# A first product's bank copied by ScalarE, and weight and activation sums moved, in a fused attention and feed-forward kernel

## The chip, the cores and the metric

The kernel runs on one core of one Trainium2 chip. The metric is the device time of one execution in microseconds. Before the change the median of three runs is 286.3 us (286.28 to 286.6). The profile that is read here is of one execution, with a span of 284.8 us from the first to the last instruction and a mean granted TensorE clock of 1.000.

## The reference

Pooled attention for 8 batches of 8 heads, 576 tokens and head size 64 (keys and values are averaged over groups of 8 tokens, which leaves 72), then a feed-forward layer with the gate h * cos(h) on all 4608 tokens:

```python
k_p = k.reshape(B, H, Sp, pool, D).mean(axis=3)          # Sp = 72, pool = 8
v_p = v.reshape(B, H, Sp, pool, D).mean(axis=3)
scores = scale * np.matmul(q, k_p.transpose(0, 1, 3, 2))
attn = softmax(scores)                                   # written out in the reference
attn_out = np.matmul(attn, v_p)

x = attn_out.transpose(0, 2, 1, 3).reshape(B * S, H * D) # 4608 x 512
h = x @ w_in                                             # 512 x 2048
g = h * np.cos(h)
out = g @ w_out                                          # 2048 x 512, float32
```

## The kernel before

The tokens are worked through in nine tiles of 512 (`t` = 0 to 8). In a tile, an "up" matmul makes h in eight blocks; ScalarE takes the cosine of each block and VectorE multiplies, which gives `g_sb`. A "down" matmul follows. While tile t is in its down matmul, the attention of batch t + 1 is computed between its parts. The order of the program is the order in which each engine works (the kernel uses a manual schedule).

From tile 1 on, the down matmul is done as a Strassen-Winograd scheme: seven products of half-size blocks instead of eight, at the price of sums of blocks. Sums of weights (`w1` to `w4`, made once, in two halves each) and of activations (`g1` to `g4`, in every tile, in two halves each) are inputs of the products:

```python
def put_weights(i, eng, ks=(1, 3, 2, 4)):
    (b11, b12), (b21, b22) = [(w[:, :, 0:HM], w[:, :, HM:]) for w in (w_out_sb[i], w_out_sb[i + 2])]
    for k in ks:
        out, x, y, op = {1: (w1, b12, b11, SUB), 3: (w3, b22, b12, SUB), 2: (w2, w3[i], b11, ADD),
                         4: (w4, b21, w2[i], SUB)}[k]
        eng.tensor_tensor(out=out[i], in0=x, in1=y, op=op)                       # L387

def put_g(k, i):
    f0, f1 = 4 * i, 4 * i + 4
    t1f1, t1f2, t2f1, t2f2 = [g_part(f, t, f0, f1) for t in range(2) for f in range(2)]
    out, x, y, op = {1: (g1, t2f1, t2f2, ADD), 2: (g2, g1[:, f0:f1], t1f1, SUB), 3: (g3, t1f1, t2f1, SUB),
                     4: (g4, t1f2, g2[:, f0:f1], SUB)}[k]
    nc.vector.tensor_tensor(out=out[:, f0:f1], in0=x, in1=y, op=op)              # L397
```

The seven products share two PSUM banks, A and Bb. Each product is 16 matmuls (L431). The first and third product both start a new sum in A, the second and fourth in Bb; between them the bank is read out:

```python
products = [
    (A, True, part(g_part(0, 0, 0, HF)), of(w_out_sb[0:2])),     # product(0)
    (Bb, True, part(g_part(1, 0, 0, HF)), of(w_out_sb[2:4])),    # product(1)
    (A, True, part(g2), of(w2)),                                 # product(2)
    (Bb, True, part(g1), of(w1)),                                # product(3)
    (A, False, part(g3), of(w3)),
    (Bb, False, part(g4), of(w_out_sb[2:4], 1)),
    (A, False, part(g_part(1, 1, 0, HF)), of(w4)),
]
# ... cut ...
            if other is None:
                (nc.scalar.copy if t >= B - 1 else nc.vector.tensor_copy)(out=out[:, p, m], in_=ps)   # L445
            else:
                nc.vector.tensor_tensor(out=out[:, p, m], in0=ps, in1=other[:, p], op=ADD)            # L447
# ... cut ...
reads = [
    lambda: each(p1, A),                  # reads[0]: the only plain copy; p_sb in the profile
    lambda: each(o1, Bb, p1, m1, 0),      # reads[1]
    lambda: each(v16, A, p1),             # reads[2]
    # ... four more, cut ...
]
```

The down part of tiles 1 to 8, with the attention between the products (`steady` is true in tiles 1 to 6, `rest` in 1 to 7). `scores_mm` are matmuls (L233), `scores_exp` is an exponential on ScalarE (L240), `values_rows` is matmuls (L295), a reciprocal and a multiplication on VectorE and a transpose by DMA:

```python
def scores_of(*parts):
    for part in parts:
        scores_mm(*part)
    for part in parts:
        scores_exp(*part)
# ... cut ...
if rest:
    exp_tables()
product(0)
product(1, 0, 2)
if steady:
    scores_of(u0, u1, u2)
elif rest:
    scores_of(ur)
product(1, 2)
if t == 1:
    put_g(2, 0)
put_gs((1, 1), (2, 1))
reads[0]()
if not steady:
    reads[1]()
put_gs((3, 1), (4, 1))
if steady:
    reads[1]()
    values_rows(*u0)
if t == 1:
    put_g(4, 0)
product(2)
reads[2]()
# ... cut: products 3 to 6 with the rest of the attention ...
```

Tile 0 has an ordinary down matmul (L370). Its attention steps and half of the weight sums stand between its matmuls; `fill` is a list of (place, step), where the place counts the 64 matmuls. The other half of the weight sums is done by GpSimd, which also pools the keys and values (L156, L162, L165, L168) and issues their loads:

```python
fill = [(2, fill[0][1]), (2, S_(0, 0)), (8, lambda: pool_v_mm(1, banks[1])),
        (8, lambda: values(t, REST, banks[2])), (8, S_(1, 0)), (8, V_(0, 1)),
        (18, S_(2, 2)), (21, V_(1, 0, later)), (26, S_(3, 1)), (32, lambda: later.pop()()),
        (32, V_(2, 2)), (40, V_(3, 0))]
# ... cut ...
    if n == 4:
        put_weights(0, nc.vector, (1,))
    elif n == 36:
        put_weights(1, nc.vector, (3,))
put_weights(1, nc.vector, (2, 4))
# ... cut: end of the tile ...
if t == 0:
    load_kv(b + 1, "k", k)
    load_q(b + 1)
    load_kv(b + 1, "v", v)
    put_weights(0, nc.gpsimd, (3, 2, 4))
    put_weights(1, nc.gpsimd, (1,))
# ... cut ...
pool_first(b + 1, "k")
if t != 1 and b + 2 < B:
    load_kv(b + 2, "k", k)
pool_rest(b + 1, "k")
```

Of the kernel before, what the change touches and what calls it, by code (L numbers as in the profile page):

```python
# [20 lines left out]
def kernel(  # L21
# [9 lines left out]
    nc = tc.nc  # L31
    B, H, S, D = q.shape
# [370 lines left out]
    def down_products(t):  # L403

        def of(w, m=0):
            return lambda fc: w[fc // 4][:, fc % 4, m * HM:(m + 1) * HM]

        def part(x):
            return lambda fc, p: x[:, fc, p * 128:(p + 1) * 128]

        apart = t == NT - 1
        if apart:
            A, Bb = [[x[:, 0:HM] for x in two] for two in (obanks, (banks[1][:, 0, :], banks[2][:, 0, :]))]
        else:
            A, Bb = [[obanks[i][:, p * HM:(p + 1) * HM] for p in range(2)] for i in (1, 0)]
        products = [
            (A, True, part(g_part(0, 0, 0, HF)), of(w_out_sb[0:2])),
            (Bb, True, part(g_part(1, 0, 0, HF)), of(w_out_sb[2:4])),
            (A, True, part(g2), of(w2)),
            (Bb, True, part(g1), of(w1)),  # L420
# [4 lines that stand above are left out]
        mms = []  # L425
        for n, (bank, first, g, w) in enumerate(products):
            order = [(fc, p) for fc in range(HF) for p in range(2)]
            if apart and n == 6:
                order.sort(key=lambda x: x[1])
            for fc, p in order:  # L430
                mms.append(lambda bank=bank, first=first, g=g, w=w, fc=fc, p=p: nc.tensor.matmul(  # L431
                    bank[p], lhsT=g(fc, p), rhs=w(fc),
                    start=(first and fc == 0 and (apart or p == 0)), stop=(fc == HF - 1 and (apart or p == 1)),
                    skip_group_check=not first))

        p1, v16, q15 = [msb.tile([128, 2, HM], FP32, name=n, tag=n, bufs=1) for n in ("p1_sb", "v_sb", "q_sb")]
        o1, o2 = [msb.tile([128, 2, d_model], FP32, name="o_two", tag="o_two", bufs=2) for _ in range(2)]
        m1, m2 = slice(0, HM), slice(HM, d_model)

        def each(out, bank, other=None, m=slice(0, HM), tk=None):  # L440

            for p in range(2) if apart else (slice(0, 2),):
                ps = bank[p] if apart else obanks[1 if bank is A else 0].rearrange("p (a m) -> p a m", a=2)
                if other is None:
                    (nc.scalar.copy if t >= B - 1 else nc.vector.tensor_copy)(out=out[:, p, m], in_=ps)  # L445
                else:
                    nc.vector.tensor_tensor(out=out[:, p, m], in0=ps, in1=other[:, p], op=ADD)  # L447
                if apart and tk is not None:
                    rows_out(t, tk, out, (p,), m, (nc.sync, nc.scalar))

        reads = [
            lambda: each(p1, A),
            lambda: each(o1, Bb, p1, m1, 0),
            lambda: each(v16, A, p1),
            lambda: each(q15, Bb, p1),
            lambda: each(o2, A, q15, m2, 1),
            lambda: (each(o1, Bb, v16, m2, 0), apart or stores.append(lambda: rows_out(t, 0, o1))),
            lambda: (each(o2, A, p1, m1, 1), apart or stores.append(lambda: rows_out(t, 1, o2))),
        ]
        return [mms[i * 2 * HF:(i + 1) * 2 * HF] for i in range(7)], reads  # L460
# [100 lines left out]
    for t in range(NT):  # L561
# [5 lines left out]
        for n, fp in enumerate(up_order(t)):  # L567
            up_mm(t, fp, 2 if n < 2 else 0)
            between = ()
            if t == 0:  # L570
                if fp == 4:
                    puts = pool_k_mm(1, obanks[0], 0, 2), pool_k_mm(1, obanks[1], 2, 4)
                elif fp in (5, 6):
                    g0 = 9 * (fp - 5)
                    puts = q_transpose_mm(1, obanks[0], g0, g0 + 5), q_transpose_mm(1, obanks[1], g0 + 5, g0 + 9)
                if fp in (4, 5, 6):
                    puts[0](vec)
                    between = ((puts[1], act),)
            up_g(t, fp, between)
            if 0 < t and 3 <= n < 6:  # L580
                put_gs(*[(k, 0) for k in (((3,), (1,), ()) if t == 1 else ((1, 2), (3,), (4,)))[n - 3]])
            if 0 < t and b < B:
                if n == 0:
                    q_transpose(b)
                    k_transpose(b)
                elif n == 2:
                    pool_rest(b, "v")
                    if b + 1 < B:
                        nc.gpsimd.tensor_copy(out=gate, in_=kk[b % 2][0:1, H - 1, 0:1])
                        load_q(b + 1)  # L590
                        load_kv(b + 1, "v", v)
            if n == 2:
                while stores:
                    stores.pop(0)()
# [17 lines left out]
            fill = [(1, lambda: scores(t, REST, banks[2])), (16, lambda: values(t, REST, banks[1]))]  # L612
        if t == 0:
            fill = [(2, fill[0][1]), (2, S_(0, 0)), (8, lambda: pool_v_mm(1, banks[1])),
                    (8, lambda: values(t, REST, banks[2])), (8, S_(1, 0)), (8, V_(0, 1)),
                    (18, S_(2, 2)), (21, V_(1, 0, later)), (26, S_(3, 1)), (32, lambda: later.pop()()),
                    (32, V_(2, 2)), (40, V_(3, 0))]
        if t == FIRST:
            early_inverses.clear()
        if t < FIRST:  # L620
            fi = 0
            for n, (ms, fc) in enumerate(mms):
                while fi < len(fill) and fill[fi][0] <= n:
                    fill[fi][1]()
                    fi += 1
                down_mm(obanks[ms % 2], ms, fc)
                if fc == FFCH - 1:
                    down_out(t, ms, obanks[ms % 2])
# [6 lines that stand above are left out]
            products, reads = down_products(t)  # L635

            def product(i, j=0, k=2 * HF):
                for mm in products[i][j:k]:
                    mm()

            later = []

            u0, u1, u2, u3 = [(b, CHUNKS[i], banks[j]) for i, j in enumerate((2, 1, 0, 1))]
            ur = (t, REST, banks[2])
# [7 lines that stand above are left out]
            def muls():  # L652
                while later:
                    later.pop(0)()

            steady, rest = b < B, t < B
# [12 lines that stand above are left out]
            reads[0]()  # L669
            if not steady:  # L670
                reads[1]()
            put_gs((3, 1), (4, 1))
            if steady:
                reads[1]()
                values_rows(*u0)
            if t == 1:
                put_g(4, 0)
            product(2)
            reads[2]()
            if steady:  # L680
                values_rows(*u1)
                values_rows(*u2)
            product(3)
            reads[3]()
            muls()
            product(4)
            reads[4]()
            muls()
            if steady:
                scores_of(ur, u3)  # L690
            product(5, 0, 4)
            if rest:
                values(*ur, later)
            product(5, 4, 12)
            muls()
            if steady:
                values_rows(*u3)
            product(5, 12)
            reads[5]()
            muls()  # L700
            product(6)
            reads[6]()
        if t < B:
            sin_tables()
        if b + 1 < B:
            if t == 0:
                load_kv(b + 1, "k", k)
                load_q(b + 1)
                load_kv(b + 1, "v", v)
                put_weights(0, nc.gpsimd, (3, 2, 4))  # L710
                put_weights(1, nc.gpsimd, (1,))
            else:

                nc.gpsimd.tensor_copy(out=gate, in_=g4[0:1, HF - 1, 0:1])  # L714
# [35 lines left out]
```

The softmax here doesn't subtract the row's maximum and nothing guards it: scores larger than these inputs give would overflow.

## Time and profile before

| quantity | value |
|---|---|
| time, median of three runs | 286.3 us |
| span of the profiled execution | 284.8 us |
| TensorE busy | 276.2 us |
| VectorE busy | 215.3 us |
| ScalarE busy | 164.4 us |
| GpSimd busy | 143.4 us |
| copy of A to p_sb on VectorE (128x512 float32), tiles 1 to 6 | 0.68 us each |
| copy of A to p_sb on ScalarE, tile 7 (same shape) | 0.57 us |
| weight sum on GpSimd | 2.13 us each, four |
| weight sum on VectorE | 0.68 to 2.28 us, four |

An engine's busy time is the sum over the whole span. The page splits the span into engines, groups of instructions by line and shape, and the chain of waits: the steps that, followed back from the last instruction, released one another. Timelines of a stretch show single instructions with start and length in microseconds; where instructions of one line follow closely they are merged, with their number behind the x. A tile's length is read from the starts of two up matmuls (L353) that follow one another.

### The profile page before, as it was taken

How to read it: one execution, taken by the hardware profiler on the slowest of the kernel's cores; microseconds unless marked ns; L12 is line 12 of the kernel's file. 1: busy time of each engine (PE TensorE's matmuls, PEld its weight loads, DVE VectorE, ACT ScalarE, POOL GpSimd, SP SyncE). 2: the span in 40 equal slices, each digit the busy share in tenths (PEclk: the TensorE clock that was granted, in tenths of full speed). 3: DMA queues.
4: the chain of work that ended last, by engine and by line, in shares of the span. 5: the costliest groups of instructions: out<-in, count | busy, mean ns of one | idle time of the engine just before them, and what ended most of it. 6: DMA issues, size and time to landing. Idle time of an engine off the chain costs nothing.

```text
span 284.8 us, 5857 instructions
## 1 busy us (share of the span) xinstructions
PE 276.2 (97%) x2360; PEld 176.4 (62%) x2360; DVE 215.3 (76%) x314; ACT 164.4 (58%) x193; POOL 143.4 (50%) x150
## 2 busy tenths in 40 slices
PE   7889999999999999999999999999999999999994
PEld 2545554446874587458745884588458844874583
DVE  5448757899957995699569956995699569856972
ACT  3787798367257735674567556655656555436600
POOL 8553069996599259924993499439900000000000
PEclk9999999999999999999999999999999999999999
DMA  7999999793939698998678969882670261015014
GB/s 154 202 206 207 207 205 216 118 199 54 145 48 161 124 221 135 138 166 169 104 135 152 186 90 160 146 172 57 119 153 3 55 128 40 0 24 126 2 37 111
DMA packets 57738, 36.12 MB, mean 127 GB/s; under 512 B 35441, under 2 KB 53361, under 8 KB 57713
## 3 DMA queue, kind: packets, MB, share of 16 engines
q0 software_dynamic: 19744, 18.07, 41.1%
q1 hardware_dynamic: 37328, 17.18, 30.0%
q10 hardware_dynamic: 640, 0.52, 0.8%
q8 instruction: 18, 0.29, 0.4%
q14 instruction: 8, 0.06, 0.1%
HBM read 36.70 MB, written 9.44 MB: 162 GB/s over the span
## 4 chain that ended last, share of the span: by engine, by line
PE 86%; DVE 6%; ACT 3%; DMA 2%; issue 1%; POOL 0%; DVEq 0%; POOLq 0%; ACTq 0%
PE bank L353 35%; PE obank L431 32%; PE obank L370 4%; PE obank L353 4%; PE bank L233 3%; DVE g_sb L367 3%; DMA q_b<-in_q_dram 2%; PE bank L295 2%; PE bank L431 2%; PE bank L268 1%; DVE w L387 1%; DVE g L397 1%; ACT cos L363 1%; ACT ex L240 1%; DVE vz L187 0%
## 5 line engine op out<-in xcount | busy, mean ns | idle before, releaser
L353 PE MATMUL bank<-xT,w_in_sb 128*128 128x512 bf16 x512 | 114.0, 379 | 0.2 <-DVE g_sb L367 0.2
L363 ACT ACTIVATE cos<-bank,half_pi 128x1024 f32<-128x1024 f32 x64 | 70.4, 1114 | 56.9 <-PE bank L353 55.0
L353 PEld LDWEIGHTS <-w_in_sb 128*128 128x128 bf16 x576 | 56.1, 98 | 66.2 <-issue 0.9
L367 DVE TENSOR_TENSOR g_sb<-bank,cos 128x1024 bf16<-128x1024 f32 x64 | 77.1, 1219 | 25.1 <-ACT cos L363 24.9
L156 POOL TENSOR_TENSOR half_sums<-kv_st 72x512 f32<-72x512 bf16 x48 | 54.7, 1165 | 0.6 <-issue 0.2
L240 ACT ACTIVATE ex<-bank 72x1024 bf16<-72x1024 f32 (+1 forms) x40 | 35.0, 929 | 34.0 <-PE bank L233 33.8
L431 PEld LDWEIGHTS <-g 128*128 128x128 bf16 x512 | 47.9, 98 | 6.1 <-issue 0.3
L431 PE MATMUL obank<-w,g 128*128 128x256 bf16 x368 | 42.7, 272 | 0.2 <-DVE p_sb L445 0.2
L431 PEld LDWEIGHTS <-g_sb 128*128 128x128 bf16 x384 | 36.8, 98 | 6.9 <-DVE g_sb L367 0.3
L162 POOL TENSOR_TENSOR half_sums<-half_sums 72x512 f32<-72x512 f32 x24 | 30.4, 1288 | 0.0
L431 PE MATMUL obank<-w_out_sb,g_sb 128*128 128x256 bf16 x240 | 28.9, 273 | 0.0
L397 DVE TENSOR_TENSOR g<-g_sb 128x1024 bf16<-128x1024 bf16 x32 | 23.3, 728 | 0.5
L714 POOL COPY gate<-g 1x1 bf16<-1x1 bf16 x5 | 0.9, 179 | 34.1 <-DVE g L397 34.1
L279 DVE TENSOR_TENSOR xT<-bank,inv 64x256 bf16<-64x256 f32 x14 | 5.9, 422 | 15.0 <-ACT inv L275 14.9
L300 DVE TENSOR_TENSOR x_rows<-bank,inv_rows 128x512 bf16<-128x512 f32 x24 | 16.6, 691 | 0.8
L431 PE MATMUL obank<-w_out_sb,g 128*128 128x256 bf16 x112 | 15.6, 273 | 0.0
L431 PE MATMUL obank<-w,g_sb 128*128 128x256 bf16 x128 | 15.3, 273 | 0.0
L370 PE MATMUL obank<-w_out_sb,g_sb 128*128 128x512 bf16 x64 | 15.2, 379 | 0.0
L353 PE MATMUL obank<-xT,w_in_sb 128*128 128x512 bf16 x64 | 15.1, 379 | 0.0
L233 PE MATMUL bank<-qT,kk 64*72 64x128 bf16 (+2 forms) x288 | 12.7, 221 | 0.1
L233 PEld LDWEIGHTS <-kk 64*72 64x72 bf16 x288 | 8.8, 110 | 5.3 <-issue 3.8
L331 ACT ACT_TABLE_LOAD x9 | 11.5, 1283 | 0.9 <-PEq L734 0.7
(103 smaller groups left out, 277.1 us busy)
## 6 DMA issues: line engine op xcount, KB each, us to landing
out_dram<-o_two SPq DMA_DIRECT2D x64, 128.0 KB, 2.4
kv_st<-in_v_dram POOLq DMA_DIRECT2D x8, 576.0 KB, 11.2
kv_st<-in_k_dram POOLq DMA_DIRECT2D x7, 576.0 KB, 8.5
q_b<-in_q_dram POOLq DMA_DIRECT2D x6, 576.0 KB, 7.5
w_in_sb<-in_moe_w_in_dram POOLq DMA_DIRECT2D x4, 512.0 KB, 13.5
w_out_sb<-in_moe_w_out_dram POOLq DMA_DIRECT2D x4, 512.0 KB, 18.2
q_b<-in_q_dram POOLq DMA_DIRECT2D x4, 288.0 KB, 12.4
g_sb<-in_k_dram SPq DMA_DIRECT2D x1, 576.0 KB, 3.6
```

The source lines that it names most:

```text
L156: nc.gpsimd.tensor_tensor(out=s[:, h:h + 2], in0=x[:, h:h + 2, 0:4, :], in1=x[:, h:h + 2, 4:8, :], op=ADD)
L162: add(out=s[:, h:h + 4, 0:2, :], in0=s[:, h:h + 4, 0:2, :], in1=s[:, h:h + 4, 2:4, :], op=ADD)
L233: nc.tensor.matmul(pair[:Sp, bank, c:c + n].rearrange("p (g n) -> p g n", n=64), lhsT=kk[b % 2][half[r], key_slot(b, h0 + i, r), 0:Sp], rh ...
L240: nc.scalar.activation(out=ex[:, 0:nh * n].rearrange("p (a n) -> p a n", a=2), in_=pair[:Sp, :, 0:nh * n // 2], func=ACTF.Exp, scale=scale ...
L300: nc.vector.tensor_tensor(out=x[0:n].rearrange("p (j a d) -> p j a d", j=KCH, a=2), in0=ps[0:n, :, 0:2 * (D + 2)].rearrange("p j (a w) -> ...
L331: nc.scalar.preload_act_table_set("natural_log_exp_and_others")
L353: nc.tensor.matmul(h[j] if h is obanks else h[:, j, :], lhsT=w_in_sb[fc // 4][:, ki, (fc % 4) * 128:(fc % 4 + 1) * 128], rhs=xT[:, ki, t * ...
L363: nc.scalar.activation(out=c, in_=ps, func=ACTF.Sin, bias=half_pi[:, :1])
L367: nc.vector.tensor_mul(out=o, in0=ps, in1=c)
L370: nc.tensor.matmul(o, lhsT=g_sb[:, fc, ms * 128:(ms + 1) * 128], rhs=w_out_sb[fc // 4][:, fc % 4, :], start=(fc == 0), stop=(fc == FFCH - 1))
L397: nc.vector.tensor_tensor(out=out[:, f0:f1], in0=x, in1=y, op=op)
L431: mms.append(lambda bank=bank, first=first, g=g, w=w, fc=fc, p=p: nc.tensor.matmul(bank[p], lhsT=g(fc, p), rhs=w(fc), start=(first and fc ...
```

## The change

Three things are moved; the arithmetic stays. The plain copy of bank A is made by ScalarE in every tile, so that VectorE has one instruction less in each of tiles 1 to 6. The four weight sums that GpSimd made are made by VectorE in tile 0, at places where it waits for others, so that GpSimd can begin to pool the next keys earlier. In tiles 1 and 2 the activation sums come later in the up matmul, and g4's first half after it, so that the products that the up matmul waits for come ahead of them.

```diff
                 if other is None:
-                    (nc.scalar.copy if t >= B - 1 else nc.vector.tensor_copy)(out=out[:, p, m], in_=ps)
+                    nc.scalar.copy(out=out[:, p, m], in_=ps)
@@
             up_g(t, fp, between)
-            if 0 < t and 3 <= n < 6:
-                put_gs(*[(k, 0) for k in (((3,), (1,), ()) if t == 1 else ((1, 2), (3,), (4,)))[n - 3]])
+
+            sums = {0: {}, 1: {5: (1,), 6: (3,)}, 2: {4: (1, 2), 5: (3,)}}.get(t, {3: (1, 2), 4: (3,), 5: (4,)})
+            put_gs(*[(i, 0) for i in sums.get(n, ())])
@@
             fill = [(2, fill[0][1]), (2, S_(0, 0)), (8, lambda: pool_v_mm(1, banks[1])),
-                    (8, lambda: values(t, REST, banks[2])), (8, S_(1, 0)), (8, V_(0, 1)),
-                    (18, S_(2, 2)), (21, V_(1, 0, later)), (26, S_(3, 1)), (32, lambda: later.pop()()),
+                    (8, lambda: values(t, REST, banks[2])),
+                    (8, lambda: put_weights(0, nc.vector, (3, 2))), (8, S_(1, 0)), (8, V_(0, 1)),
+                    (18, S_(2, 2)), (18, lambda: put_weights(0, nc.vector, (4,))),
+                    (18, lambda: put_weights(1, nc.vector, (1,))), (21, V_(1, 0, later)), (26, S_(3, 1)), (32, lambda: later.pop()()),
                     (32, V_(2, 2)), (40, V_(3, 0))]
@@
             reads[0]()
             if not steady:
                 reads[1]()
-            put_gs((3, 1), (4, 1))
+            put_g(3, 1)
+            if t == 1:
+                reads[1]()
+            if t <= 2:
+                put_g(4, 0)
+            put_g(4, 1)
             if steady:
-                reads[1]()
+                if t > 1:
+                    reads[1]()
                 values_rows(*u0)
-            if t == 1:
-                put_g(4, 0)
             product(2)
@@
                 load_kv(b + 1, "v", v)
-                put_weights(0, nc.gpsimd, (3, 2, 4))
-                put_weights(1, nc.gpsimd, (1,))
```

## The prediction

> **What bounds the kernel now.** I read the page's header parts first, then the idle time of TensorE, then the chain of waits, and only then the timelines of single tiles. The page's first part says which engine is full:
>
> ```profile
> PE 276.2 (97%) x2360; PEld 176.4 (62%) x2360; DVE 215.3 (76%) x314; ACT 164.4 (58%) x193; POOL 143.4 (50%) x150
> ```
>
> TensorE (PE) is busy for 276.2 of 284.8 us; 8.6 us of idle is all that any rearrangement of the other engines can win. I asked for the busy time by stretch, with the borders put where each tile's up matmul starts. Columns after the border: length of the stretch, then busy time and instruction count of PE, of weight loads, of VectorE (DVE), ScalarE (ACT), GpSimd (POOL), then clock and DMA.
>
> ```profile
> 0.00:17.40 17.40, 13.80 (x173) 7.44 (x174) 9.47 (x22) 10.71 (x14) 11.37 (x23) 1.00 1.03 183
> ...
> 53.40:83.10 29.70, 29.24 (x257) 19.50 (x256) 27.01 (x35) 17.05 (x19) 24.39 (x23) 1.00 0.73 118
> 83.10:112.20 29.10, 29.07 (x258) 19.30 (x256) 23.25 (x35) 17.05 (x19) 20.02 (x21) 1.00 0.95 150
> ...
> 141.10:170.06 28.96, 28.96 (x258) 19.41 (x256) 23.03 (x35) 17.05 (x19) 19.56 (x21) 1.00 0.81 142
> ...
> 254.60:284.80 30.20, 26.03 (x176) 16.98 (x174) 19.70 (x30) 9.61 (x11) 0.00 (x0) 1.00 0.32 70
> ```
>
> Idle TensorE lies in the first stretch (17.40 - 13.80 = 3.6 us) and the last (30.20 - 26.03 = 4.2 us), neither of which the change touches. Tile 4 (141.10 to 170.06) has none. Tile 1 (53.40 to 83.10) has 0.46 us, tile 2 has 0.03 us. By the starts of the up matmuls in the PE timeline (53.20, 82.98, 112.00, 140.95 us) tile 1 takes 29.78 us, tile 2 29.02 and tile 3 28.95. So the change can win at most 0.83 us in tile 1 and 0.07 in tile 2, some 0.9 us or 0.3%.
>
> The chain of waits over 53 to 76 us shows where tile 1 loses it. Columns: start, length, what.
>
> ```profile
> 54.09 2.21 DVE w L387
> ...
> 56.32 1.65 DVE w L387
> ...
> 65.68 1.90 PE bank L353 x8
> ...
> 71.91 0.61 DVE p_sb L445
> 72.52 0.04 issue
> 72.56 1.91 PE obank L431 x16
> ```
>
> Two weight sums hold VectorE back by 3.9 us, its products come late, and TensorE waits twice for 0.23 us: at 65.68 for a g_sb product, at 72.56 for the copy of the first product's bank. The second wait also tells a dependency that matters below: **the third product (L431, x16, operand w2) cannot start before p_sb is copied**, because it starts a new sum in the bank that the copy reads. It follows the copy's end by 0.04 us.
>
> In steady tiles this copy is just in time. Tile 4, the timeline of all engines from 156 to 160 us, where the last line is cut by the window (start, busy time, engine, line, operation):
>
> ```profile
> 156.09 1.28 ACT L331 ACT_TABLE_LOAD   x1
> ...
> 157.39 2.84 ACT L240 ACTIVATE ex<-bank 72x1024 bf16<-72x1024 f32 x3
> ...
> 158.70 0.68 DVE L445 COPY p_sb<-obank 128x512 f32<-128x512 f32 x1
> 159.27 0.41 PE L295 MATMUL bank<-vz,ex 72*128 72x65 bf16 x8
> ...
> 159.52 0.71 PE L431 MATMUL obank<-w,g 128*128 128x256 bf16 x5
> ```
>
> VectorE's copy ends at 159.38 and the third product starts at 159.52: 0.14 us of slack. And ScalarE is in the middle of three exponentials until 160.23. The reader should hold those two numbers side by side.
>
> **What the Trainium skill says.** "PSUM — Partial Sum Buffer", section Engine vs sequencer instructions: "ScalarE/VectorE/GpSimdE queues are strict FIFO." The trace agrees as far as it can: in each tile the records of an engine stand in the order of the program. "SBUF — State Buffer", section Who interferes with whom, has a VectorE instruction with two SBUF inputs exclude a GpSimd instruction that reads SBUF, the later one waiting for the whole of the other. The trace agrees: the weight sum takes 0.68 us at 36.1 while GpSimd is idle, but 2.28 at 54.0 and 1.65 at 56.3, while GpSimd runs its float32 sums (L162, L165). "ScalarE: Activation LUTs", section Table sets: the hidden batching unit, lists copy among the functions of every set, so a copy on ScalarE needs no table load; in tile 7, where ScalarE already makes it, it follows the exponential with no load between.
>
> **The change part by part.**
>
> *The copy on ScalarE.* In tiles 7 and 8 it is there already; so six tiles change, 1 to 6. It takes 0.68 us off VectorE and puts this on ScalarE (row of tile 7):
>
> ```profile
> 244.23 0.59 ACT L240 ACTIVATE ex<-bank 72x512 bf16<-72x512 f32 x1
> 244.72 0.57 ACT L445 COPY p_sb<-obank 128x512 f32<-128x512 f32 x1
> ```
>
> It lasts 0.57 us and starts 0.10 before the recorded end of the exponential ahead (244.23 + 0.59 - 244.72). In tile 7 there is one exponential ahead of it, in tiles 1 to 6 there are three: in the program scores_of(u0, u1, u2) issues all of them before reads[0]. That order is not changed. So in tile 4 the copy starts at 157.39 + 2.84 - 0.10 = 160.13, ends at 160.70, and the third product may start at 160.74 instead of 159.52: **TensorE stands still for 1.22 us.** Tile 3 gives the same (exponentials at 128.44, product at 130.57: 131.79 - 130.57 = 1.22). TensorE has no idle time later in the tile in which to make that up, and the next tile's table load, exponentials and copy all follow TensorE, so it comes back each tile. Tiles 3 to 6: 4 x 1.22 = 4.9 us.
>
> *Tile 2.* A steady tile plus the stall, 28.95 + 1.22 = 30.17, against 29.02 now: +1.15. The later g4 sum takes away the 0.07.
>
> *Tile 1.* Sums moved later (g1 and g3 after the sixth and seventh block of the up matmul, one after the other, instead of the fourth and fifth) let the products of blocks 5 to 7 go ahead; the sum at 62.68, which cost 1.81 us beside GpSimd, goes to a quieter place. That should remove the wait at 65.68. If tile 1 then keeps the pace of tile 3, where the exponentials start 128.44 - 112.00 = 16.44 after the up matmul, they start at 69.64, the copy ends at 69.64 + 2.84 - 0.10 + 0.57 = 72.95, and the third product starts at 72.99 against 72.56: +0.43. If nothing is recovered they start at 70.03 and it is +0.82. I take +0.6.
>
> *Weight sums on VectorE.* Four GpSimd sums of 2.13 us go, four VectorE sums come, 0.68 each with GpSimd idle, 4 x 0.68 = 2.7 us. Two go into the hole between 39.88 and 41.81 (1.93 us against 1.36), two into that between 43.20 and 44.54 (1.34 against 1.36). Just about fits; the copy of the first output block behind the second hole may come 0.1 late, and with it TensorE at 47.57, where it already follows a VectorE product. I put +0.1 on it, up to +0.3.
>
> *GpSimd freed.* This looks like 8.5 us (four sums from 38.55 to 47.14), but the first pooling sum behind them needs keys whose transfer was issued at 25.98 and took 20.5 us to land: 46.5. GpSimd starts its pooling 0.6 us earlier at most, so its float32 sums still meet the two weight sums left at the end of tile 0, and those stay near 3.9 us.
>
> Sum: 4.9 + 1.15 + 0.6 + 0.1 = 6.7 us; 286.3 + 6.7 = 293.0 us.
>
> **The rivals.** (a) *The relief counts, the copy is free.* If ScalarE made the copy before or between the exponentials, TensorE would lose nothing and up to 0.9 us would be won: 285.4 to 286.3. For it: ScalarE is only 58% busy and idle after its exponentials. Against: program order, and that the bank is wanted 0.7 us before the exponentials end. Average load hides this. (b) *The freed GpSimd brings transfers forward* and they collide with the transposes and stores. The late key transfer speaks against it; effect under 0.5 us either way. (c) *VectorE becomes the bound in tile 0*: two weight sums more before the end of tile 0 lengthen the chain of attention values. VectorE is busy 9.23 of 14.5 us there; even if all of the second pair fell on the path, 1.4 us, total near 294.3. (d) *The stall is smaller than worked out*, because TensorE catches up elsewhere. The windows show no idle in tiles 3 to 6, so nothing can be caught up.
>
> **Range and chances.** The main term is 1.22 us with about 0.1 either way, six times: 0.6 us. Tile 1 adds 0.2, tile 0 up to 0.3 either side. Range 291.9 to 293.9 us. The border of 2% slower lies at 286.3 x 1.02 = 292.0, 1.0 below my figure, so most of the range is beyond it: slower by over 2% 0.85, within 2% 0.13. Faster by over 2% would need more than the 0.9 us to be won: 0.02.
>
> **What would show it.** Right: p_sb's copy on ScalarE directly behind the three exponentials, ending some 3.3 us after the first of them started; in tiles 1 to 6 a wait of TensorE L431 on ACT p_sb L445 of about 1.2 us each (7 us in all, tile 1 included); tiles 3 to 6 each 30.2 us long; TensorE's busy time unchanged at 276 and the span about 291.5. Tile 1: no wait for g_sb. Tile 0: weight sums of 0.7 us. Wrong: a copy that stands before an exponential, a third product that starts without it, or a tile 3 of 28.95 us. If tile 3 is 30.2 and the total still differs, the fault is in tiles 0 to 2.

## The result, and the profile after

The changed kernel takes 295.59 us (median of four runs, 295.3 to 295.94) against 286.45 us for the kernel before: a ratio of 1.0314 (95% interval 1.0291 to 1.0337), 9.1 us slower. The predicted direction holds; the predicted time, 293.0 us with a range up to 293.9, was too low. The profiled execution has a span of 293.5 us, 8.7 more than before. The first part of the page after:

```profile
PE 276.9 (94%) x2360; PEld 176.8 (60%) x2360; DVE 214.0 (73%) x312; ACT 167.1 (57%) x199; POOL 133.7 (46%) x146
```

VectorE has become lighter (215.3 to 214.0 us), GpSimd too (143.4 to 133.7), TensorE does the same work in 8.7 us more. The totals would be read as relief; only TensorE's idle time tells. Its waits over the whole span (who waited for whom: total, times, longest), the two that are new:

```profile
PE obank L431 <- ACT p_sb L445: 6.2, 6, 1.1
PE bank L353 <- DVE o_two L447: 1.6, 1, 1.6
```

Six waits for ScalarE's copy, and one wait of an up matmul, which was not foreseen. By stretch, cut where the up matmuls of tiles 1, 2, 3 and 4 and of the last tile start (columns as in the prediction):

```profile
53.08:83.25 30.17, 29.17 (x257) 19.51 (x256) 25.29 (x35) 17.50 (x20) 23.43 (x22) 1.00 0.74 117
83.25:115.41 32.16, 29.33 (x259) 19.29 (x257) 24.13 (x36) 17.51 (x20) 22.91 (x26) 1.00 0.97 147
115.41:145.58 30.17, 29.10 (x257) 19.48 (x258) 20.99 (x31) 17.51 (x20) 18.28 (x20) 1.00 0.84 130
145.58:175.75 30.17, 29.10 (x259) 19.50 (x256) 22.60 (x34) 17.51 (x20) 19.71 (x21) 1.00 0.81 137
262.73:293.50 30.77, 26.21 (x178) 17.10 (x175) 19.71 (x30) 9.60 (x11) 0.00 (x0) 0.98 0.31 69
```

Tiles 1, 3 and 4 (and 5 and 6) are 30.17 or 30.18 us long: the 28.95 of a steady tile before and 1.22. Tile 2 is 32.16. The last stretch is 30.77, where it was 30.32 before (from 254.43 to 284.75). Tile 4, ScalarE's and TensorE's instructions from 162 to 166 us, the last cut by the window:

```profile
162.02 2.84 ACT L240 ACTIVATE ex<-bank 72x1024 bf16<-72x1024 f32 x3
...
163.90 0.41 PE L295 MATMUL bank<-vz,ex 72*128 72x65 bf16 x8
...
164.74 0.58 ACT L445 COPY p_sb<-obank 128x512 f32<-128x512 f32 x1
...
165.38 0.82 PE L431 MATMUL obank<-w,g 128*128 128x256 bf16 x6 [1.07 <-ACT p_sb L445]
```

The copy stands behind the three exponentials and ends at 165.32; the third product follows at 165.38, and the bracket says that TensorE was idle for 1.07 us before it. The tile grows by 1.22: in the row of before, the records of the value matmuls (L295) and of the third product overlap by 0.16 us (159.27 + 0.41 - 159.52), and behind a wait that overlap is lost.

Tile 2's extra length lies at its end. There the profile names the VectorE sum of L447 as what the up matmul waited for. The transfers issued between 108.0 and 108.2 us say something else (output, queue, count, size, median us from issue to landing):

```profile
kv_st<-in_k_dram POOLq DMA_DIRECT2D x1, 576.0 KB, 8.9
xT<-x_rows SPq DMA_TRANSPOSE x1, 7.1
```

The transpose of the third chunk of batch 3's tokens into xT starts at 108.07 and lands 7.1 us later, at 115.2; the up matmul of tile 3, which reads these tokens, starts at 115.41. Before, the same transpose, issued between 107.03 and 107.6, took 2.5:

```profile
xT<-x_rows SPq DMA_TRANSPOSE x1, 2.5
```

What differs is the load of keys (kv_st, 576 KB). Before, it was issued 0.65 us behind the last transpose:

```profile
107.03 1.22 SPq L304 DMA_TRANSPOSE xT<-x_rows  x1
107.68 0.84 POOL L115 DMA_DIRECT2D kv_st<-in_k_dram  x1 [0.30 <-POOL half_sums L156]
```

After, the two are issued together:

```profile
108.07 1.22 SPq L304 DMA_TRANSPOSE xT<-x_rows  x1
108.09 0.84 POOL L115 DMA_DIRECT2D kv_st<-in_k_dram  x1 [0.30 <-POOL half_sums L156]
```

That suggested the second theory below.

### The profile page after: what moved, and what is told of

Its sections match the earlier page's. It is cut to its first block, busy times and chain, and to the rows that moved or that the text cites. A ratio compares the mean times of both kernels' runs of the same rounds, so it can differ in the third digit from the quotient of the medians.

```text
span 293.5 us, 5838 instructions
## 1 busy us (share of the span) xinstructions
PE 276.9 (94%) x2360; PEld 176.8 (60%) x2360; DVE 214.0 (73%) x312; ACT 167.1 (57%) x199; POOL 133.7 (46%) x146
## 4 chain that ended last, share of the span: by engine, by line
PE 77%; ACT 10%; DVE 6%; issue 3%; DMA 2%; POOL 0%; DVEq 0%; POOLq 0%; ACTq 0%
PE bank L353 36%; PE obank L431 24%; ACT ex L240 6%; PE obank L353 5%; PE obank L370 4%; DVE g_sb L367 3%; ACT cos L363 3%; DMA q_b<-in_q_dram 2%; PE bank L431 2%; PE bank L233 1%; PE bank L295 1%; PE bank L268 1%; ACT p_sb L445 1%; DVE o_two L447 1%; DVE g L397 1%
## 5 line engine op out<-in xcount | busy, mean ns | idle before, releaser
L367 DVE TENSOR_TENSOR g_sb<-bank,cos 128x1024 bf16<-128x1024 f32 x64 | 77.3, 1220 | 28.6 <-ACT cos L363 28.4
L397 DVE TENSOR_TENSOR g<-g_sb 128x1024 bf16<-128x1024 bf16 x32 | 22.2, 693 | 0.4
L447 DVE TENSOR_TENSOR o_two<-obank,p_sb 128x512 f32<-128x512 f32 (+1 forms) x16 | 10.5, 654 | 4.8 <-ACT p_sb L445 3.8
```

The source lines that it names most:

```text
L367: nc.vector.tensor_mul(out=o, in0=ps, in1=c)
```

## The experiments

**Theory 1**: the copy's place behind three exponentials is the loss in each of tiles 1 to 6. **Theory 2**: tile 2's further loss of some 2 us is a consequence of it: the stall delays the transposes, but hardly the key load that GpSimd issues, and the two meet. **Rivals**: a copy on ScalarE is dear wherever it stands; or the moved sums cost the time.

**The copy back on VectorE**, all else as changed:

```diff
-                    nc.scalar.copy(out=out[:, p, m], in_=ps)
+                    (nc.scalar.copy if t >= B - 1 else nc.vector.tensor_copy)(out=out[:, p, m], in_=ps)
```

> The changed kernel with the copy of the first product's bank back on VectorE in tiles 1 to 6; the moved sums stay. Theory 1 (the copy's place behind three exponentials is the whole loss, and the longer tile 2 is only its consequence): the third product no longer waits for ScalarE, tiles 3 to 6 are 28.95 us again, tile 1 stays at the steady length (0.8 us less than before), so about 285.6 us. Rival (the weight sums on VectorE or the moved activation sums cost the 2 us more in tile 2): tile 2 stays near 31 us and the time is 287.5 to 288 us.

Measured: 286.61 us, ratio to before 1.0008 (0.9993 to 1.0024). The whole loss is gone, and so is the long tile 2 (29.17). The expected gain of 0.9 us is not there. By the starts of the up matmuls, tile 1 is 29.35, tile 2 29.17, tile 3 29.27. In tile 1 the copy on VectorE still holds TensorE up (0.2 us). In tile 3 one sum of VectorE lasts longer:

```profile
120.69 1.19 DVE L397 TENSOR_TENSOR g<-g_sb 128x1024 bf16<-128x1024 bf16 x1
```

Its usual time is 0.68, and GpSimd pools values (L168, 120.06 to 121.33) beside it. The products behind it come late and TensorE waits 0.3 us for g_sb. What the move of the sums won in tile 1 (29.78 - 29.35 = 0.43 us), tile 2 (0.15 longer) and tile 3 (0.32 longer) took back.

**The copy alone on ScalarE** (the kernel before with the reverse of that edit):

> The kernel before with nothing but the copy on ScalarE in tiles 1 to 6. Theory 1 with theory 2 (the copy costs 1.22 us in each of six tiles, and the later transposes of tile 2 meet the load of keys): 286.4 + 0.8 + 5 x 1.22 + 2.0 = 295.3 us, with a wait of near 1.6 us of the up matmul at the start of tile 3. Rival (the 2 us come from the moved sums): 293.3 us and no such wait.

Measured: 296.35 us, ratio 1.0368 (1.0312 to 1.0425). The copy alone makes at least the full loss. Whether the rest of the change reduces it is not shown: the intervals of the two ratios overlap. The 295.3 expected was exceeded in tile 2 and at the end (a last stretch of 31.0 us). Tile 1 is 30.58 long, tile 2 32.88, tiles 3 to 6 30.17 or 30.18. Here the profile names the wait at tile 3's start by its true cause:

```profile
PE bank L353 <- DMA xT<-x_rows: 2.5, 1, 2.5
```

**The key load of tile 2 later**, the changed kernel otherwise:

```diff
-            if t != 1 and b + 2 < B:
+            if t not in (1, 2) and b + 2 < B:
                 load_kv(b + 2, "k", k)
             pool_rest(b + 1, "k")
-            if t == 1:
+            if t in (1, 2):
                 load_kv(b + 2, "k", k)
```

> The changed kernel, with the load of the keys in tile 2 issued after the rest of the key pooling, some 4 us later, as tile 1 does it already. Theory 2 (the last transpose of x_rows takes 7.1 us to land because this load starts in the same moment): that transpose lands in about 3 to 4 us, the up matmul of tile 3 does not wait, tile 2 is 30.2 to 30.4 us long instead of 32.16, and the time is 293.7 us. Rival (the transposes are slow from the query and value loads under way already, or something else holds the up matmul): stays at 295.6 us. The waits for the copy stay in both.

Measured: 293.36 us, ratio 1.0244 (1.0221 to 1.0268), so 2.2 us less than the changed kernel's 295.59. Tile 2 is 30.41 long. GpSimd issues the load at 111.48 now, and the transpose issued between 107.8 and 108.2 lands in

```profile
xT<-x_rows SPq DMA_TRANSPOSE x1, 2.7
```

with no wait of the up matmul. Theory 2 holds: 32.16 - 30.41 = 1.75 us of tile 2 is the meeting of the two transfers. The Trainium skill, "DMA: Bandwidth & Descriptors", section Issuing engines are not separate DMA queues, says that transfers of different engines run on the same 16 DMA engines and interleave; 2.5, 7.1 and 2.7 us for one transpose agree.

**The copy one exponential earlier**:

```diff
-                for part in parts:
+                for n, part in enumerate(parts):
+                    if n == copy_before:
+                        reads[0]()
                     scores_exp(*part)
@@
-                scores_of(u0, u1, u2)
+                scores_of(u0, u1, u2, copy_before=2)
@@
-            reads[0]()
+            if not steady:
+                reads[0]()
```

> The changed kernel, with the copy on ScalarE ahead of the last of the three exponentials in tiles 1 to 6. Theory 1: the copy ends one exponential (0.92 us) earlier, the wait of the third product falls from 1.22 us to 0.30 us a tile, 285.6 + 6 x 0.30 = 287.4 us, up to 289 us if the tile 2 transposes still meet the key load. Rival (a copy on ScalarE is dear in itself, by its way to TensorE or by sharing PSUM): the wait stays near 1.2 us and the time near 295 us.

Measured: 287.94 us, ratio 1.0052 (1.0035 to 1.0069). Tiles 3 to 6 are 29.26 to 29.27 long: 0.32 above 28.95, where 0.30 was expected. A copy on ScalarE is thus not dear in itself; its place is. Tile 2 is 29.50, with no late transpose.

**The copy ahead of all exponentials, and ahead of the second** (`copy_before=0` and `1` in the same edit):

> The changed kernel, with ScalarE's copy ahead of all three exponentials in tiles 1 to 6. Theory 1: the bank is copied about 1.5 us before the third product wants it, no wait for ScalarE, tiles 3 to 6 at 28.95 us, tile 1 at 29.0 to 29.3, tile 2 at 29.2, no late transpose: about 286.0 us, of which 0.4 us lies after the last work as in the other kernels with this copy. Rival (the exponentials, each now 0.47 us later, become what the value products wait for): tiles of 29.3 to 29.5 us and 288 us.

> The same with the copy between the first and the second exponential. Theory 1: it ends two exponentials earlier than in the changed kernel, 1.22 - 1.83 is below zero, so no wait, tiles of 28.95 us, about 286.0 us; the first exponential keeps its place. If it differs from the copy ahead of all three, the first exponential's time matters to the value products.

Measured: 286.61 us, ratio 1.0 (0.9989 to 1.0011), and 286.62 us, ratio 0.9994 (0.9977 to 1.001). In both, tiles 3 to 6 are 28.95 and tile 2 is 29.17. Neither reaches the 286.0 us expected. With three, two, one and no exponential ahead of the copy a steady tile is 30.17, 29.27, 28.95 and 28.95 us long. Tile 1 differs, 28.96 in the one and 29.80 in the other. In the latter the first of the two late weight sums lasts 2.78 us beside GpSimd, in the former 1.29. That is no merit of the copy's place. In the former, tile 0 was 0.5 us longer (36.38 against 35.85), 0.4 of it a wait for a load of w_out, so that the sums met less of GpSimd's work; and the latter's profile is of an execution of 287.41 us, 0.8 above its median. Between the two, no difference in the time can be measured.

**The weight sums alone** (the kernel before with that part of the diff) **and the activation sums alone**:

> The kernel before with only the four weight sums moved from GpSimd to VectorE. If GpSimd waits for the keys in any case: first pooling sum 0.3 to 0.6 us earlier, nothing gained in tiles 1 and 2, time 286.3 to 286.7 us. Rival (the freed GpSimd alone makes the loads earlier and the pooling faster): 285.5 us. Rival (VectorE too full in tile 0): 287 us or more, with tile 0 longer.

> The kernel before with only the activation sums of tiles 1 and 2 moved. From the run with the copy undone: tile 1 0.4 us shorter (29.35), tile 2 0.15 us longer, so 286.3 us. If tile 3's extra 0.3 us there comes from a VectorE sum that meets a GpSimd sum, it may be there or not, as the two engines happen to stand: up to 286.6 us.

The activation sums alone: 286.69 us, ratio 1.0002 (0.9985 to 1.0019), as expected, with tile 1 at 29.68 rather than 29.35. The weight sums alone: 294.19 us, ratio 1.0262 (1.0236 to 1.0288), as none of the three readings had it. Tile 0 is not longer; tile 1 takes 37.38 us. From VectorE's and GpSimd's timelines between 73 and 82 us:

```profile
74.01 4.47 POOL L156 TENSOR_TENSOR half_sums<-kv_st 72x512 f32<-72x512 bf16 x4
78.45 2.47 POOL L162 TENSOR_TENSOR half_sums<-half_sums 72x512 f32<-72x512 f32 x2
81.00 1.60 POOL L165 TENSOR_TENSOR ring<-half_sums 72x512 bf16<-72x512 f32 x1
...
75.09 6.38 DVE L397 TENSOR_TENSOR g<-g_sb,g 128x1024 bf16<-128x1024 bf16 x1
```

One sum (g4's first half) lasts 6.38 us instead of 0.68. It ends 0.5 us after the first short gap in GpSimd's row of six sums. In the kernel before the same sum, at 75.06, lasts 0.87, and GpSimd's row begins at 74.24, a quarter of a microsecond later against it:

```profile
74.24 4.92 POOL L156 TENSOR_TENSOR half_sums<-kv_st 72x512 f32<-72x512 bf16 x4 [0.23 <-issue]
...
75.06 0.87 DVE L397 TENSOR_TENSOR g<-g_sb,g 128x1024 bf16<-128x1024 bf16 x1
```

The quarter is an idle time of GpSimd ahead of its row (0.23, in the bracket); why it is missing in the run with the weight sums alone was not tested. TensorE's fifth product then waits 5.4 us for a VectorE sum that stands behind this one.

**The weight sums with that one activation sum moved**, as the change has it:

```diff
-            put_gs((3, 1), (4, 1))
+            put_g(3, 1)
+            if t == 1:
+                put_g(4, 0)
+            put_g(4, 1)
@@
-            if t == 1:
-                put_g(4, 0)
```

> The kernel with only the weight sums moved, in which one sum of tile 1 (g4, first half) lasted 6.38 us beside GpSimd's pooling, now with that sum ahead of g4's second half, for which GpSimd's pooling waits, as the change has it. If GpSimd's chain of pooling sums keeps the VectorE sum out: no sum over 2.3 us in tile 1, tile 1 at 29.8 us instead of 37.4, time 286.6 us. Rival (the weight sums themselves make tile 1 longer, by a late operand): tile 1 stays above 35 us and the time near 294 us.

Measured: 286.76 us, ratio 1.0004 (0.999 to 1.0019). GpSimd's pooling waits for g4's second half, so the first half now runs before it, in 0.68 us. That the meeting with the pooling made the 6.38 us is shown. Tile 1 is 30.94, not the expected 29.8: one of the late weight sums lasts 3.32 us here, in an execution of 288.2 us, 1.4 above the median. Moving g4's first half looked like a detail of the change; without it the weight sums cost 7.6 us, with it nothing that can be measured.

**Six spare ScalarE copies.** The last stretch remained: 30.7 to 31.0 us in the kernels with the copy on ScalarE in all six tiles, 30.3 to 30.4 in all without.

```diff
                 scores_of(u0, u1, u2)
+                nc.scalar.copy(out=spare, in_=half_pi[0:1, 0:1])
```

> The kernel before, with one more ScalarE copy of a single element in each of tiles 1 to 6, behind the exponentials, whose result nobody reads. All kernels with the six real copies on ScalarE took 30.7 to 31.0 us from the last up matmul to the end, all others 30.3. If the mere number of ScalarE's instructions does it (a fetch of instructions that falls into the last stores), this one takes 30.7 or more and 286.9 us in all; if it is something else in those kernels, 30.3 and 286.5 us.

Measured: 286.61 us against 286.38 for the kernel before beside it, ratio 1.001 (1.0 to 1.002). The last stretch is 30.86 us against 30.32. The median, 0.2 us higher, is at the border of what can be measured and below the 286.9 expected. So six more ScalarE instructions, copies of a bank or spare ones, go with 0.4 to 0.5 us at the end of the profiled executions. TensorE's and VectorE's last work ends alike in both, 26.2 and 26.7 us into the stretch; ScalarE's last store is issued 27.26 us into it instead of 26.98. Among the transfers of the last 16 us, there is one that the kernel before does not have there:

```profile
q14 instruction: 1, 0.01, 0.2%
```

It is a fetch of instructions. All seven kernels with six more ScalarE instructions have it 27.9 to 28.4 us into the last stretch, while the last stores are under way; in the six others it comes only after 30.7, behind the end. That fits the longer end; that the fetch is its cause is argued from these traces, not tested by itself.

**A version that uses what was found**: the copy on ScalarE ahead of the exponentials in tiles 1 to 3, on VectorE in tiles 4 to 6, and tile 2's activation sums placed as tile 1's.

```diff
-                    nc.scalar.copy(out=out[:, p, m], in_=ps)
+                    (nc.scalar.copy if t <= 3 or t >= B - 1 else nc.vector.tensor_copy)(out=out[:, p, m], in_=ps)
@@
-            sums = {0: {}, 1: {5: (1,), 6: (3,)}, 2: {4: (1, 2), 5: (3,)}}.get(...)
+            sums = {0: {}, 1: {5: (1,), 6: (3,)}, 2: {5: (1,), 6: (3,)}}.get(...)
@@
-                scores_of(u0, u1, u2)
+                scores_of(u0, u1, u2, copy_before=0 if t <= 3 else None)
@@
-            if t == 1:
+            if t <= 2:
                 put_g(2, 0)
             put_gs((1, 1), (2, 1))
-            reads[0]()
+            if t > 3:
+                reads[0]()
```

> The changed kernel, with the copy on ScalarE ahead of the exponentials in tiles 1 to 3 only and on VectorE in tiles 4 to 6, and with tile 2's activation sums placed as tile 1's. Tiles 1 to 3 should all be near 28.95 us, which is 0.9 us less than before in tiles 1 and 2 together; 0.4 us of that may go after the last work, as in all kernels with more copies on ScalarE. 285.6 to 286.1 us; if tile 2's sums then come late for the third product, 286.6 us.

Measured: 286.14 us, ratio 0.9979 (0.9967 to 0.9991): faster than the kernel before by 0.2%. Its stretches, tiles 1, 2 and 3:

```profile
52.98:81.94 28.96, 28.91 (x257) 19.42 (x256) 24.55 (x35) 17.52 (x20) 22.52 (x22) 1.00 0.80 121
81.94:110.90 28.96, 28.86 (x257) 19.41 (x257) 22.23 (x34) 17.52 (x20) 19.72 (x22) 1.00 0.93 149
110.90:140.12 29.22, 28.89 (x256) 19.28 (x256) 22.86 (x34) 17.52 (x20) 21.04 (x22) 1.00 0.89 146
```

Tiles 1 and 2 have reached the steady length; tile 3 lost 0.27. Of the 0.88 us won in the two, some 0.5 remain in the median (286.14 against 286.65).

## Why the prediction was right, and where it was wrong

Lengths of the profiled executions, before and after, against the terms of the sum:

| term | predicted | measured |
|---|---|---|
| tile 0 and what is before it | +0.1 | -0.12 (53.20 to 53.08) |
| tile 1 | +0.6 | +0.39 (29.78 to 30.17) |
| tile 2 | +1.15 | +3.14 (29.02 to 32.16) |
| tiles 3 to 6 | +4.9 | +4.9 (4 x 1.22) |
| tile 7 | 0 | -0.01 |
| last tile and end | 0 | +0.45 (30.32 to 30.77) |
| sum | 6.7 | 8.7 |

The rest of the 9.1 us is the scatter of single executions around the medians. Against the 6.7 us predicted, tile 2 came out 2.0 us longer and the end 0.45; tiles 0 and 1 came out 0.2 shorter each.

**The stall** was right in kind and in size: 1.22 us a tile, from the durations of a tile that already had the copy on ScalarE and from the program's order. The runs with the copy at four places show that its place makes the stall, and not the copy as such. The waits come to 6.2 us, not to the 7 named as a sign: each is some 0.15 short by the lost overlap, and tile 1's is only 0.83.

**Tile 1** recovered all that the moved sums could give: 30.17 is a steady tile and the stall, so the bound of +0.43 came true and not the middle of the two bounds. Its exponentials start at 69.52, 16.44 us after the up matmul, the pace of tile 3 that the bound assumed. One wait for g_sb is left (0.17 us, ahead of the scores), against the sign "no wait for g_sb"; it costs nothing, as ScalarE's row is what the third product waits for.

**Tile 2 is the step that failed**: "a steady tile plus the stall", +1.15 us, where +3.14 were measured. It took the stall to shift everything behind it alike. GpSimd's pooling, and with it the key load, is released by g4, which does not wait for the copy; the transposes come from VectorE's multiplications behind the copy. Against the start of tile 2's up matmul the key load moved from 107.68 - 82.98 = 24.70 to 108.09 - 83.25 = 24.84 us, the last transpose from 107.03 - 82.98 = 24.05 to 108.07 - 83.25 = 24.82. The margin of 0.65 us between the two was gone. The late key load shows the price, 1.75 us.

Rival (b), "effect under 0.5 us either way", named such a meeting, but looked for it from the other side, from a freed GpSimd that issues its loads earlier. That reason was rightly dismissed: with the copy alone, GpSimd still makes its four weight sums, and TensorE waits 2.5 us for the transpose. What I did not ask is what the stall does to the order of transfers.

The price falls on tile 2 alone. Tile 3's up matmul needs the third chunk of batch 3, while tile 4's needs only the first two of batch 4 (256 of its 576 tokens). In tiles 3 and 4 of the changed kernel the third transpose lands late too, 9.3 us after its issue, and nothing waits for it. In tile 1 the program issues the key load only after the pooling. The remaining excess of tile 2, 30.41 - 28.95 - 1.22 = 0.24, is VectorE: "the later g4 sum takes away the 0.07" was wrong too. With the sums as the change places them, tile 2 is 29.17 without any stall, 0.15 longer than before, since two sums stand just ahead of a g_sb multiplication that TensorE then waits for (0.2 us).

**The end**, +0.45, was not in the sum at all; the prediction said that the change does not touch the last stretch. The spare copies show that it comes with six more ScalarE instructions.

**Weight sums** in tile 0 fitted their holes as worked out: 0.69 us each with GpSimd idle, waiting for keys until 46.88; the two left at the end still took 2.17 and 1.64. That they were harmless in the change was luck: the prediction did not see that, without the move of g4's first half, they cost 7.6 us.

## What to carry to other kernels

An instruction moved to an idle engine takes its place in that engine's order: compare the time at which its result is wanted with the end of what stands ahead of it, not with the engine's busy share. If that makes a stall, list everything that the stall delays and everything that it doesn't, and look which transfers or sums then meet: here a margin of 0.65 us hid 1.75 us. Where the profile names a releaser whose result the waiting instruction does not use, look at the landings of the transfers.

## What the runs showed of the hardware that was not expected

A VectorE sum of two SBUF operands was kept out by GpSimd not for one instruction, but for a row of six that followed one another without a gap: 6.38 us instead of 0.68. The same sum lost only 0.2 us in the kernel before, where GpSimd's row stood 0.25 us later.

With six ScalarE instructions more, of one element each, the last stretch of the profiled execution was about 0.5 us longer (30.32 to 30.86).

A transpose of 128 tokens landed in 2.5 us where a load of 576 KB was issued 0.65 us behind it, and in 7.1 us where the load was issued 0.02 us behind it.
